# First k on ScalarE's DMA queue, second q on the software queue, and S ahead of Y, at the head of a fused retention and gated-MLP kernel

## The chip, the cores and the metric

One core of one Trainium2 chip. The metric is the device time of one execution in microseconds (us), median of several. A traced span is shorter than the time of the same execution (207.8 against 209.6 us for the kernel before).

## The reference

```python
# q, k, v: (4 batches, 8 heads, 768 steps, 64), fp32
gamma = 1.0 - 2.0 ** (-5.0 - np.arange(8))
for t in range(768):
    state = gamma * state + outer(k[t], v[t])      # per batch and head
    y[t] = q[t] @ state / 8
x = y as (3072, 512);  h = x @ w_in                # (512, 2048)
out = (h * cos(h)) @ w_out                         # (2048, 512)
```

The kernel works in chunks of 128 steps. A "pair" is one chunk of two batches (b = 0 and 1); there are 12 pairs. Per pair: convert q and k to bf16, transpose (T), form scores (A), multiply by the mask (M), form the output half by half (Y), update the state (S). Then comes the MLP: up-projection, h cos(h), down-projection.

## The kernel before

Lines with `clk.run` or `banks.give` are left out of these cuts without a mark. The loads at the start:

```python
load(nc.sync, 0, ("q0", "k0", "q1"))      # pair 0; SyncE's hardware queue, 256 KB each
nc.gpsimd.iota(...); nc.gpsimd.iota(...)
load(nc.gpsimd, 0, ("k1",))               # GpSimd's software queue
load(nc.gpsimd, 1, ("q0", "q1"))          # pair 1
load_k(1)
load(nc.gpsimd, 0, ("v0", "v1"))
# ... cut: constants ...
load(nc.gpsimd, 1, ("v0", "v1"))
load_w_in_0(); load_w_in(1)
# ... GpSimd converts most of the v of pairs 0 and 1 (vs) ...
```

The work on pair 0 (`warm(n)` issues n filler matmuls of 128x512 on zeros; `clk.run` only steers a model that picks PSUM banks, it issues nothing):

```python
warm(8)
conv_q(0, nc.vector, (0,))       # VectorE: q of b = 0 to bf16
conv_k(0, True)                  # ScalarE: k of b = 0, then of b = 1
stage_t(0, 0, 2)                 # PE: 4 transposes of q, 2 fillers, 4 of k; VectorE copies the bank out, "evicts" it (qkt)
conv_q(0, nc.vector, (1,))       # VectorE: q of b = 1, "the second q"
warm(3)
stage_m(0, stage_a(0, 0))        # A on PE, mask multiplies (am) on VectorE
# ... cut ...
```

The end of the head, and the first matmuls of the MLP:

```python
stage_m(1, stage_a(1, 0))
half_y(0, 0)
stage_m(1, stage_a(1, 1))
stage_s(0, nc.scalar.copy)       # S of pair 0, then its state copies (stb) on ScalarE
half_y(0, 1)
warm(3)
half_y(1, 0)                     # needs stb and am of pair 1
half_y(1, 1)
stage_s(1, nc.scalar.copy)
first_f()                        # first up-projection
```

## Time and profile before

| | before |
|---|---|
| time, first 3 runs | 209.31 us (209.24 to 209.52) |
| traced span | 207.8 us |
| first up-projection matmul | 16.94 us |
| from there to the end | 190.9 us |

From the page of the kernel before, part 1 (busy us, share of the span, count of instructions):

```profile
PE 200.2 (96%) x1646; PEld 112.9 (54%) x1646; DVE 113.3 (55%) x188; ACT 114.3 (55%) x193; POOL 102.2 (49%) x118
```

The waits of PE from 16.9 us to the end, kernel before; after these two header lines the list is empty:

```profile
core 0 of [0], span 207.8 us
engine line waited for: us in total, times, longest us
```

So PE is an unbroken stream from the first up-projection on. What can be won by this change lies in the first 17 us, and it is won only if that matmul starts earlier.

The timeline of the kernel before (start us, duration us, engine, line, operation, tiles, count, and in brackets the idle time before it with what ended it), VectorE:

```profile
3.91 0.69 DVE L195 TENSOR_TENSOR qk<-qf,gq 128x512 bf16<-128x512 f32 x1 [1.23 <-DMA qf<-in_q_dram]
7.42 0.69 DVE L214 TENSOR_SCALAR qkt<-bank 128x512 uint32<-128x512 uint32 x1 [2.81 <-PE bank L230]
8.02 0.68 DVE L195 TENSOR_TENSOR qk<-qf,gq 128x512 bf16<-128x512 f32 x1
...
13.41 2.47 DVE L266 TENSOR_TENSOR am<-bank,mask 128x512 bf16<-128x512 f32 x4
```

The first line is the first q, the second the first eviction of transposes, the third the second q. From 7.42 us no VectorE instruction has a bracket: it never idles until the last mask multiply ends at 13.41 + 2.47 = 15.88 us. I call this VectorE's chain. Its start was held by the first k, as ScalarE's timeline shows:

```profile
6.31 1.14 ACT L208 CAST qk<-kf 128x512 bf16<-128x512 f32 x2 [1.86 <-DMA kf<-in_k_dram]
...
14.44 1.19 ACT L313 CAST stb<-st_ps 64x512 bf16<-64x512 f32 x2
```

PE at the end of the head, kernel before (L301 is S, L413 fillers, L279 and L284 the Y halves, L360 the first up-projection):

```profile
13.95 0.44 PE L301 MATMUL st_ps<-vs,qk 128*64 128x64 bf16 x16
14.23 0.39 PE L284 MATMUL bank<-am,vs 128*64 128x128 bf16 x8
14.55 0.82 PE L413 MATMUL bank<-gt 128*128 128x512 bf16 x3
15.30 0.61 PE L279 MATMUL bank<-qkt,stb 128*64 128x128 bf16 x2
...
16.54 0.47 PE L301 MATMUL st_ps<-vs,qk 128*64 128x64 bf16 x16
16.94 0.30 PE L360 MATMUL bank<-xt,w_in 128*128 128x256 bf16 x1
```

The state copies end at 15.63 us, and the Y halves of pair 1 run behind them. Between the end of VectorE's chain and the up-projection lie 16.94 - 15.88 = 1.06 us.

The DMA queues between 4 and 5 us, kernel before (q0 is the software queue, with packets of up to 4 KB; q1 is SyncE's hardware queue, with 256-byte packets):

```profile
q0 software_dynamic: 62, 0.22, 72.1%
q1 hardware_dynamic: 254, 0.06, 27.9%
```

### The profile page before, as it was taken

How to read it: one execution, taken by the hardware profiler on the slowest of the kernel's cores; microseconds unless marked ns; L12 is line 12 of the kernel's file. 1: busy time of each engine (PE TensorE's matmuls, PEld its weight loads, DVE VectorE, ACT ScalarE, POOL GpSimd, SP SyncE). 2: the span in 40 equal slices, each digit the busy share in tenths (PEclk: the TensorE clock that was granted, in tenths of full speed). 3: DMA queues.
4: the chain of work that ended last, by engine and by line, in shares of the span. 5: the costliest groups of instructions: out<-in, count | busy, mean ns of one | idle time of the engine just before them, and what ended most of it. 6: DMA issues, size and time to landing. Idle time of an engine off the chain costs nothing.

```text
span 207.8 us, 4176 instructions
## 1 busy us (share of the span) xinstructions
PE 200.2 (96%) x1646; PEld 112.9 (54%) x1646; DVE 113.3 (55%) x188; ACT 114.3 (55%) x193; POOL 102.2 (49%) x118
## 2 busy tenths in 40 slices
PE   7689999999999999999999999999999999999993
PEld 2257554558897555546544465544465444444452
DVE  4591984464957563869874367853357244443000
ACT  6677873247997336577743754653554653553120
POOL 8999238399999999999995230000000000000000
PEclk9999999999999999999999999999999999999999
DMA  6999999999999999859899841161101101110212
GB/s 159 340 245 200 216 248 286 331 256 344 243 240 293 271 247 263 246 191 225 245 178 102 234 83 50 57 101 50 50 3 50 50 14 40 50 52 18 83 75 80
DMA packets 36644, 33.83 MB, mean 163 GB/s; under 512 B 26768, under 2 KB 29072, under 8 KB 36624
## 3 DMA queue, kind: packets, MB, share of 16 engines
q0 software_dynamic: 7808, 20.98, 39.6%
q1 hardware_dynamic: 28672, 12.49, 26.7%
q8 instruction: 13, 0.21, 0.5%
q10 hardware_dynamic: 144, 0.10, 0.1%
q14 instruction: 7, 0.06, 0.1%
HBM read 27.26 MB, written 6.29 MB: 161 GB/s over the span
## 4 chain that ended last, share of the span: by engine, by line
PE 92%; DVE 3%; DMA 2%; issue 1%; ACT 1%; SPq 0%; DVEq 0%
PE bank L379 39%; PE bank L338 32%; PE bank L349 7%; PE bank L257 3%; PE bank L279 3%; PE bank L284 3%; DMA kf<-in_k_dram 2%; PE bank L396 2%; PE st_ps L301 1%; DVE am L266 1%; PE bank L230 1%; PE bank L360 1%; PE bank L367 1%; DVE qkt L214 1%; DVE qk L195 1%
## 5 line engine op out<-in xcount | busy, mean ns | idle before, releaser
L331 DVE TENSOR_TENSOR gt<-bank,cosb 128x512 bf16<-128x512 f32 x96 | 64.8, 688 | 61.9 <-ACT cosb L327 61.6
L327 ACT ACTIVATE cosb<-bank,halfpi 128x512 bf16<-128x512 f32 x96 | 65.2, 688 | 49.9 <-PE bank L338 45.4
L379 PE MATMUL bank<-w_out_sb,gt 128*128 128x512 bf16 x368 | 89.6, 379 | 0.0
L338 PE MATMUL bank<-xt,w_in 128*128 128x512 bf16 x304 | 75.3, 380 | 0.0
L379 PEld LDWEIGHTS <-gt 128*128 128x128 bf16 x368 | 35.5, 98 | 41.2
L338 PEld LDWEIGHTS <-w_in 128*128 128x128 bf16 x304 | 33.7, 114 | 30.9
L266 DVE TENSOR_TENSOR am<-bank,mask 128x512 bf16<-128x512 f32 x48 | 30.4, 681 | 3.9 <-PE bank L257 3.9
L386 ACT COPY ob<-bank 128x512 f32<-128x512 f32 x23 | 13.4, 587 | 18.3 <-PE bank L379 18.3
L202 POOL TENSOR_TENSOR vs<-vf,gk 128x512 bf16<-128x512 f32 x21 | 21.4, 1042 | 3.2 <-PE st_ps L301 3.1
L132 POOL DMA_DIRECT2D vf<-in_v_dram x23 | 20.2, 883 | 5.2 <-DMA w_out_sb<-in_moe_w_out_dram 5.2
L195 POOL TENSOR_TENSOR qk<-qf,gq 128x512 bf16<-128x512 f32 x18 | 18.5, 1049 | 7.7 <-issue 4.8
L132 POOL DMA_DIRECT2D kf<-in_k_dram x21 | 18.9, 900 | 1.8 <-DMA w_out_sb<-in_moe_w_out_dram 1.6
L208 ACT CAST qk<-kf 128x512 bf16<-128x512 f32 x24 | 13.8, 615 | 9.5 <-DMA kf<-in_k_dram 9.5
L288 ACT CAST xt<-bank 128x512 bf16<-128x512 f32 x24 | 13.0, 588 | 8.0 <-PE bank L284 7.8
L132 POOL DMA_DIRECT2D qf<-in_q_dram x18 | 16.2, 901 | 0.6 <-DMA w_in<-in_moe_w_in_dram 0.6
L349 PE MATMUL bank<-xt,w_in 128*128 128x256 bf16 x128 | 14.7, 273 | 0.0
L349 PEld LDWEIGHTS <-w_in 128*128 128x128 bf16 x128 | 13.8, 114 | 0.4
L284 PE MATMUL bank<-am,vs 128*64 128x128 bf16 x192 | 11.7, 220 | 0.0
L279 PEld LDWEIGHTS <-stb 128*64 128x64 bf16 x160 | 8.8, 109 | 4.3 <-issue 3.1
L279 PE MATMUL bank<-qkt,stb 128*64 128x128 bf16 x160 | 10.7, 222 | 0.1
L284 PEld LDWEIGHTS <-vs 128*64 128x64 bf16 x192 | 10.0, 110 | 0.5 <-issue 0.4
L313 DVE CAST stb<-st_ps 64x512 bf16<-64x512 f32 x12 | 8.2, 684 | 2.7 <-PE st_ps L301 2.6
(46 smaller groups left out, 85.8 us busy)
## 6 DMA issues: line engine op xcount, KB each, us to landing
vf<-in_v_dram POOLq DMA_DIRECT2D x23, 256.0 KB, 6.5
out_dram<-ob SPq DMA_DIRECT2D x23, 256.0 KB, 2.2
kf<-in_k_dram POOLq DMA_DIRECT2D x21, 256.0 KB, 6.7
qf<-in_q_dram POOLq DMA_DIRECT2D x18, 256.0 KB, 5.6
w_out_sb<-in_moe_w_out_dram POOLq DMA_DIRECT2D x4, 512.0 KB, 12.7
qf<-in_q_dram SPq DMA_DIRECT2D x6, 256.0 KB, 8.3
w_in<-in_moe_w_in_dram POOLq DMA_DIRECT2D x3, 512.0 KB, 7.9
kf<-in_k_dram POOLq DMA_DIRECT2D x1, 512.0 KB, 6.0
```

The lines of the kernel that those rows point to most:

```text
L132: eng.dma_start(out=t[SLOT[p]][b], in_=src[2 * bp + b, :, ds(c * C, C)].rearrange("h t d -> t h d"))
L195: eng.tensor_tensor(out=qk[p % NB][:, b, 0], in0=qf[SLOT[p]][b], in1=bc(gq, p % NC), op=ALU.mult)
L202: eng.tensor_tensor(out=vs[p % NB][:, b], in0=vf[SLOT[p]][b], in1=bc(gk, p % NC), op=ALU.mult)
L208: nc.scalar.copy(out=qk[p % NB][:, b, 1], in_=kf[SLOT[p]][b])
L266: nc.vector.tensor_tensor(out=am[p % 2][b][j], in0=ap[j], in1=mask.unsqueeze(1).to_broadcast([128, HP, 128]), op=ALU.mult)
L279: nc.tensor.matmul(yp[ts(j, 64), a, :], lhsT=stb[p % 2][:, b, a, ts(j, 64)], rhs=qt(n, b, a), start=True, stop=False, skip_group_check=True)
L284: nc.tensor.matmul(yp[ts(j, 64), a, :], lhsT=vs[n][:, b, 2 * a + j, :], rhs=am[p % 2][b][j][:, a, :], start=(c == 0), stop=True, skip_grou ...
L327: nc.scalar.activation(out=cb, in_=bank, func=AF.Sin, bias=halfpi)
L331: nc.vector.tensor_tensor(out=out, in0=bank, in1=cb, op=ALU.mult)
L338: nc.tensor.matmul(bank, lhsT=w_in_t(i, f), rhs=xt[g % 2][:, i, :], start=(i == 0), stop=(i == KIN - 1))
L349: nc.tensor.matmul(bank[:, ts(e, 256)], lhsT=w_in_t(i, f + e), rhs=xt[g % 2][:, i, ts(hf, 256)], start=(i == 0 and e == 0), stop=(i == KIN ...
L379: nc.tensor.matmul(bank, lhsT=gt[g % 2][:, f, ts(j, 128)], rhs=w_out_sb[:, f, :], start=(f == 0), stop=(f == KOUT - 1))
```

## The change

Its intent: bring the first k sooner, by issuing it from ScalarE beside the first q; let the second q take the software queue and the first q of pair 1 the free place on SyncE's; and run S of pair 0 early, so that its state copies are done before the Y halves of pair 1 need them.

```diff
-    load(nc.sync, 0, ("q0", "k0", "q1"))
+    load(nc.scalar, 0, ("k0",))
+    load(nc.sync, 0, ("q0",))
+    load(nc.sync, 1, ("q0",))
@@
-    load(nc.gpsimd, 0, ("k1",))
-    load(nc.gpsimd, 1, ("q0", "q1"))
+    load(nc.gpsimd, 0, ("k1", "q1"))
+    load(nc.gpsimd, 1, ("q1",))
@@
     stage_m(1, stage_a(1, 0))
+    stage_s(0, nc.scalar.copy)
+    clk.run("pe", 0.0, 13.0)
+    stage_m(1, stage_a(1, 1))
     half_y(0, 0)
-    clk.run("pe", 0.0, 12.4)
-    stage_m(1, stage_a(1, 1))
-    stage_s(0, nc.scalar.copy)
     half_y(0, 1)
-    warm(3)
+    warm(1)
     half_y(1, 0)
+    warm(2)
     banks.give(spare, clk.pe)
     half_y(1, 1)
     stage_s(1, nc.scalar.copy)
```

## The prediction

> **What bounds the kernel now.** By the page's busy shares PE is busy 96% of 207.8 us. The waits of PE list none after 16.9 us: from there PE is one unbroken stream. So the change can only move the start of that stream, the first up-projection matmul at 16.94 us; a microsecond won there is a microsecond of total.
>
> **What bounds the first 17 us.** The timeline shows: k of batch 0 is second on SP's queue and lands at about 6.3 us. ScalarE copies it (0.62 us), PE transposes, and at 7.42 us VectorE starts. From 7.42 to 15.88 us VectorE never idles (fourteen conversions, evictions and mask multiplies of 0.68 us): the bound in the middle. PE has 1.06 us of work behind the last mask multiply: the second Y half of pair 1 and its S. The state copies on ScalarE (14.44 to 15.63 us) also hold the first Y half of pair 1 back to 15.67 us.
>
> **What the change does.**
> 1. k0 goes to a second hardware queue beside q0. The DMA view gives the hardware queue 1849 packets of 256 bytes by 4.0 us, so the two (2048 packets) are nearly through when the software queue's 4 KB packets begin (62 in the next microsecond, 254 for the hardware queue). The Trainium skill, page "DMA: Bandwidth & Descriptors", section "Queues, rings and completion order", says that the engines round-robin between queues packet by packet; the trace agrees: those 62 packets took 72% of the engines. I expect q0 later (4.3 to 5.2 us against 3.9), k0 earlier (4.6 to 5.8 against 6.3), and the first eviction of transposes at 6.2 to 7.0 us instead of 7.42.
> 2. The second q moves from third on the hardware queue (used at 8.02 us) to second on the software queue. The second software transfer was used by ScalarE at 8.00 us before. Its landing, about 7.9 us, then holds VectorE's second conversion, which stands in order ahead of the mask multiplies. So most of point 1 turns into idle time of VectorE. Net shift of its chain: 0.1 us, between -0.3 and +0.7.
> 3. S of pair 0 ahead of Y: state copies end at about 14.95 us instead of 15.63, so the first Y half of pair 1 runs before VectorE's last mask multiply ends. Behind that end remain the second half (0.45 us) and S (0.4 us): 0.85 instead of 1.06 us, a gain of 0.2 us.
>
> Sum: 0.3 us, and a little in case point 2 lands early.
>
> **Predicted time: 208.9 us**, 8 in 10 between 208.2 and 209.5. Chances: faster by over 2% 0.01 (4.2 us out of a 17 us head), within 2% 0.98, slower 0.01.
>
> **What would show it.** In the timeline: k's first copy before 6 us; first eviction of transposes before 7.1 us; VectorE then idle until the second q's DMA releases it at about 7.9 us, and unbroken to about 15.8 us; state copies done by 15 us; first up-projection matmul at about 16.6 us; no PE wait after it.
>
> **What would make it wrong.** If the second q lands on the software queue at 7 us, the chain gains up to 0.8 us. If it comes at 8.5 us or later, the change loses. If three queues in turn delay q0 beyond 6 us, point 1 gains nothing. If the new order of bank use makes PE wait, point 3's gain is lost.

## The result, and the profile after

The changed kernel took 209.03 us (median of 6, 208.88 to 209.78), the kernel before 209.38 us (median of 6). The ratio is 0.9989, 95% interval 0.9968 to 1.001. A ratio here is the mean time of one kernel's runs over that of the other's of the same rounds, so it is not quite the ratio of the medians quoted. Executions over 1.5% slower than the fastest of the same kernel are left out of the means. The interval holds 1; a later set of rounds (e0 below) gave 0.9981, 0.9968 to 0.9994, a gain of about 0.2%, whose interval does not hold 1.

| | before | after |
|---|---|---|
| first q converted from | 3.91 us | 4.49 us |
| first k copied from | 6.31 us | 4.92 us |
| first eviction (start of the chain) | 7.42 us | 7.16 us |
| second q converted from | 8.02 us | 7.77 us |
| end of VectorE's chain | 15.88 us | 15.64 us |
| first up-projection matmul | 16.94 us | 16.67 us |
| from there to the end | 190.9 us | 190.9 us |

Both profiled executions were slower than the medians of their kernels: 209.60 us against 209.38 before, 209.35 against 209.03 after. The table compares two single executions, and its 0.27 us at the last matmul agrees with the 0.35 us of the medians only roughly.

From the page of the kernel after, part 1:

```profile
PE 199.5 (96%) x1624; PEld 113.5 (55%) x1646; DVE 113.3 (55%) x188; ACT 114.1 (55%) x193; POOL 102.3 (49%) x118
```

(1624 matmuls against 1646 weight loads: some records are missing. The waits of PE after 16.6 us list only four gaps without a releaser, of 0.2 us at most, where they fell out.)

VectorE's timeline, kernel after:

```profile
4.49 0.69 DVE L197 TENSOR_TENSOR qk<-qf,gq 128x512 bf16<-128x512 f32 x1 [1.80 <-DMA qf<-in_q_dram]
7.16 0.69 DVE L216 TENSOR_SCALAR qkt<-bank 128x512 uint32<-128x512 uint32 x1 [1.98 <-PE bank L232]
7.77 0.68 DVE L197 TENSOR_TENSOR qk<-qf,gq 128x512 bf16<-128x512 f32 x1
...
13.16 2.48 DVE L268 TENSOR_TENSOR am<-bank,mask 128x512 bf16<-128x512 f32 x4
```

The first k came 1.39 us earlier, as its copy on ScalarE shows, and the state copies start 0.93 us earlier:

```profile
4.92 0.62 ACT L210 CAST qk<-kf 128x512 bf16<-128x512 f32 x1 [0.38 <-DMA kf<-in_k_dram]
...
13.51 1.18 ACT L315 CAST stb<-st_ps 64x512 bf16<-64x512 f32 x2 [1.78 <-PE st_ps L303]
```

Yet the first eviction moved by only 0.26 us. The k copy ended at 5.54 us, and PE transposed k only at 6.49 us. PE's timeline, kernel after (L415 are fillers, L232 transposes; the second transposes are those of k):

```profile
5.24 0.61 PE L232 MATMUL bank<-ident,qk 128*128 128x128 bf16 x4 [0.45 <-DVE qk L197]
5.64 1.06 PE L415 MATMUL bank<-gt 128*128 128x512 bf16 x2
6.49 0.63 PE L232 MATMUL bank<-ident,qk 128*128 128x128 bf16 x4
...
14.62 0.37 PE L281 MATMUL bank<-qkt,stb 128*64 128x128 bf16 x2 [0.25 <-DVE am L268]
...
15.31 0.60 PE L415 MATMUL bank<-gt 128*128 128x512 bf16 x2
15.85 0.25 PE L281 MATMUL bank<-qkt,stb 128*64 128x128 bf16 x2
...
16.32 0.42 PE L303 MATMUL st_ps<-vs,qk 128*64 128x64 bf16 x16
16.67 0.52 PE L362 MATMUL bank<-xt,w_in 128*128 128x256 bf16 x3
```

Two fillers stood between the transposes of q and those of k and took 1.06 us by their modelled ends (the transposes of k started 0.85 us after the first filler), because PE was still at its slow pace: 0.43 us from one filler to the next, against 0.22 us later. The slow pace is that of PE's granted clock. The views print a clock of 1.00 for every stage, but they count time without a clock record as full; the record itself, which I read from the packed trace, has its first entry (full clock) at 7.18 us here and at 4.23 us in the kernel before, and the pace rises at these moments. And at the end the first Y half of pair 1 did run before the chain's end, but two fillers then filled PE until 15.85 us, 0.2 us beyond that end. Behind the chain lie 16.67 - 15.64 = 1.03 us, against 1.06 before.

The DMA queues between 4 and 5 us, kernel after (q10 is ScalarE's hardware queue):

```profile
q1 hardware_dynamic: 831, 0.21, 93.2%
q10 hardware_dynamic: 305, 0.07, 33.5%
q0 software_dynamic: 2, 0.01, 2.0%
```

The software queue moved 62 packets in this microsecond before, 2 after. Its first packet came at 4.91 instead of 3.96 us. Still the second q, second in that queue, had landed at 7.28 us (I read landings from the semaphore events of the trace), where before, third on the hardware queue, it landed at 7.51 us.

### The profile page after: what moved, and what is told of

It reads as the page before. It is cut to its first block, busy times and chain, and to the rows that moved or that the text cites. A ratio compares the mean times of both kernels' runs of the same rounds, so it can differ in the third digit from the quotient of the medians.

```text
span 207.6 us, 4155 instructions
## 1 busy us (share of the span) xinstructions
PE 199.5 (96%) x1624; PEld 113.5 (55%) x1646; DVE 113.3 (55%) x188; ACT 114.1 (55%) x193; POOL 102.3 (49%) x118
## 4 chain that ended last, share of the span: by engine, by line
PE 91%; DVE 4%; DMA 2%; issue 1%; DVEq 0%
PE bank L381 38%; PE bank L340 32%; PE bank L351 7%; PE bank L281 3%; PE bank L259 3%; PE bank L286 2%; DMA qf<-in_q_dram 2%; DVE am L268 2%; PE bank L398 2%; PE bank L232 1%; PE st_ps L303 1%; DVE qk L197 1%; DVE qkt L216 1%; PE bank L362 1%; PE bank L369 1%
## 5 line engine op out<-in xcount | busy, mean ns | idle before, releaser
L381 PE MATMUL bank<-w_out_sb,gt 128*128 128x512 bf16 x359 | 88.5, 379 | 0.7 <-issue 0.3
L340 PE MATMUL bank<-xt,w_in 128*128 128x512 bf16 x294 | 74.3, 380 | 0.7 <-issue 0.3
L351 PE MATMUL bank<-xt,w_in 128*128 128x256 bf16 x128 | 14.7, 273 | 0.0
```

The source lines that it names most:

```text
L340: nc.tensor.matmul(bank, lhsT=w_in_t(i, f), rhs=xt[g % 2][:, i, :], start=(i == 0), stop=(i == KIN - 1))
L351: nc.tensor.matmul(bank[:, ts(e, 256)], lhsT=w_in_t(i, f + e), rhs=xt[g % 2][:, i, ts(hf, 256)], start=(i == 0 and e == 0), stop=(i == KIN ...
L381: nc.tensor.matmul(bank, lhsT=gt[g % 2][:, f, ts(j, 128)], rhs=w_out_sb[:, f, :], start=(f == 0), stop=(f == KOUT - 1))
```

## The experiments

Twelve kernels in three sets of four, five rounds each, each set on one chip. All results were correct. Medians come from 5 or 6 runs. "First F" is the start of the first up-projection matmul; "behind" is First F less the end of VectorE's chain. Ratios are to the kernel before in the same set.

| run | second q converted | chain's end | First F | behind | time us | ratio (95%) |
|---|---|---|---|---|---|---|
| e0 the change again | 7.83 | 15.70 | 16.73 | 1.03 | 208.96 | 0.9981 (0.9968-0.9994) |
| e1 loads only | 7.17 | 15.04 | 16.09 | 1.05 | 208.80 | 0.9981 (0.9968-0.9995) |
| e2 order only | 7.85 | 15.72 | 16.75 | 1.03 | 209.36 | 1.0001 (0.9989-1.0013) |
| e3 no fillers in T | 7.30 | 15.17 | 16.21 | 1.04 | 208.86 | 0.9978 (0.9966-0.9990) |
| e5 e3, second q on SyncE | 6.80 | 14.68 | 16.22 | 1.54 | 208.86 | 0.9958 (0.9920-0.9997) |
| e6 e3, one hardware queue | 7.46 | 15.33 | 16.37 | 1.04 | 209.20 | 0.9978 (0.9935-1.0021) |
| e7 e3, no end fillers | 7.43 | 15.31 | 16.09 | 0.78 | 208.65 | 0.9948 (0.9909-0.9987) |
| e8 e3, S of pair 1 ahead | 7.16 | 15.04 | 15.57 | 0.53 | 208.42 | 0.9939 (0.9900-0.9977) |
| e9 e8 and e5 together | 6.76 | 14.88 | 15.62 | 0.74 | 208.20 | 0.9950 (0.9927-0.9974) |
| e10 e8, S of pair 0 late | 7.11 | 14.98 | 16.04 | 1.06 | 208.86 | 0.9980 (0.9957-1.0004) |
| e11 change, one more filler | 7.44 | 15.31 | 16.34 | 1.03 | 208.91 | 0.9982 (0.9957-1.0008) |
| e12 e9, weights later | 6.73 | 15.01 | 16.40 | 1.39 | 208.31 | 0.9960 (0.9934-0.9987) |

The columns from the trace are of one execution each, the times of five or six. In the later two sets the kernel before scattered widely (up to 211.7 us, and 215.5 us in one run, which the ratios leave out), so the medians say more there than the ratios, and a difference between sets of less than about 0.2 us should not be trusted.

### e0: the change again

Edit: none.

> The changed kernel unaltered, for a second profile and a tighter interval. Theory P (PE's fillers): the first eviction of transposes starts at 7.16 us in the first profile because PE, still at its slow pace, has two filler matmuls (1.06 us) between the transposes of q and those of k; where PE reaches its fast pace earlier in this execution the eviction starts up to 0.5 us earlier. Theory Q (second q): the second q's landing sets the start of VectorE's second conversion. Both: about 0.3 us below the kernel before, first up-projection matmul at 16.3 to 16.7 us. It also tells whether the software queue's first packets come at 4.9 us again (3.9 us in the kernel before).

Measured: 208.96 us. The profile repeats the first one: fillers at 5.82 and 6.24 us, 0.42 us apart, first eviction at 7.23 us, First F at 16.73 us. But this profiled execution was the slowest of its five: 209.41 us, the others 208.85 to 209.00. In the first set too the profiled one took 209.35 us and four of the others 208.9 to 209.1 (the fifth 209.78). So both profiles of the changed kernel show an execution with a late pace (clock record from 7.18 and 6.93 us), and most executions were about 0.4 us faster. That these had their fast pace early is an inference: they have no trace.

### e1: the loads only

Edit: the change's new loads in the kernel before.

> The new loads with the old order of PE's work. If the two parts add up as predicted, VectorE's second conversion starts at about 7.8 us, its chain ends at about 15.6 us, and the first up-projection matmul at about 16.7 us: 0.25 us below the kernel before, the same as the whole change, since the order alone would only save PE work behind the chain's end. If the order carries the gain, 16.9 us and no gain.

Measured: 208.80 us, First F at 16.09 us. In this execution PE was fast at 5.34 us, so the fillers cost little, and VectorE did what the prediction said, waiting for the second q. VectorE's timeline of e1:

```profile
6.20 0.69 DVE L216 TENSOR_SCALAR qkt<-bank 128x512 uint32<-128x512 uint32 x1 [1.17 <-PE bank L232]
7.17 0.69 DVE L197 TENSOR_TENSOR qk<-qf,gq 128x512 bf16<-128x512 f32 x1 [0.28 <-DMA qf<-in_q_dram]
```

Only it landed at 7.14 us, not 7.9. The loads carry the whole gain of the change: 208.80 us without the new order, 208.96 with it, in the same set. The expected 16.7 us was missed because the chain came 0.6 us earlier than I thought. Its runs also fall into two groups: 208.74 to 208.82 (four) and 209.26, 209.34 (two).

### e2: the order only

Edit: the change's new order of PE's work with the old loads.

> The old loads with the new order of PE's work. Predicted 0.2 us of gain: state copies done by about 15.0 us, the first Y half of pair 1 before VectorE's last mask multiply ends (15.9 us), first up-projection matmul at about 16.75 us. Rival: the two fillers between the Y halves (0.60 us, and 0.54 us from their start to the next matmul in the changed kernel) give the gain back, and it starts at 16.9 us, no gain.

Measured: 209.36 us against 209.26 for the kernel before, ratio 1.0001. The rival was right: behind the chain lie 1.03 us, no fewer than before. First F came at 16.75 us, as the theory said, but for another reason: the chain itself came 0.16 us earlier in this execution than in the first profile of the kernel before. VectorE's timeline of e2 shows more:

```profile
6.27 0.69 DVE L214 TENSOR_SCALAR qkt<-bank 128x512 uint32<-128x512 uint32 x1 [1.72 <-PE bank L230]
7.85 0.69 DVE L195 TENSOR_TENSOR qk<-qf,gq 128x512 bf16<-128x512 f32 x1 [0.89 <-DMA qf<-in_q_dram]
```

With the same old loads as the kernel before, the first k was there at 5.16 us instead of 6.31, and the chain still did not start earlier than 7.85 us: it waited for the second q. In the old loads the second q was a bound close behind the first k, so a faster k alone could move the second conversion from 8.02 us only to 7.85 us (here) or about 7.5 us (the second q's landing in the first profile). The new loads brought both: the second q landed at 7.1 to 7.5 us on the software queue, against 7.5 and 7.8 us as third on the hardware queue.

### e3: no fillers between the first transposes

```diff
-    stage_t(0, 0, 2)
+    stage_t(0, 0)
```

> The changed kernel without the two filler matmuls between the first transposes of q and of k. Theory P: the first eviction starts at about 6.1 us instead of 7.16, VectorE's second conversion then waits for the second q until about 7.3 us, and the first up-projection matmul comes at about 16.2 us, 0.4 to 0.5 us earlier than in the changed kernel. Theory Q: the second conversion stays at 7.8 us and nothing moves. A loss would mean that PE stays at its slow pace for longer without the fillers.

Measured: 208.86 us, and all five runs within 208.85 to 208.98; First F at 16.21 us. VectorE's timeline of e3:

```profile
6.29 0.69 DVE L216 TENSOR_SCALAR qkt<-bank 128x512 uint32<-128x512 uint32 x1 [1.11 <-PE bank L232]
7.30 0.69 DVE L197 TENSOR_TENSOR qk<-qf,gq 128x512 bf16<-128x512 f32 x1 [0.32 <-DMA qf<-in_q_dram]
```

Theory P holds for the profiled executions of the change: the fillers delayed the chain. Theory Q holds for what comes next: without them VectorE waits for the second q (whether that also holds First F, e5 tests). In the median e3 wins only 0.1 us over e0 (208.96). No run of e3 is near 209.4 us, but with five runs, against one such in five of e0 and two of 209.3 us or more in six of the first set, it is not shown that the slow group is gone.

### e5: the second q back on SyncE's queue

```diff
-    load(nc.sync, 1, ("q0",))
+    load(nc.sync, 0, ("q1",))
-    load(nc.gpsimd, 0, ("k1", "q1"))
-    load(nc.gpsimd, 1, ("q1",))
+    load(nc.gpsimd, 0, ("k1",))
+    load(nc.gpsimd, 1, ("q0", "q1"))
```

> Against e3 (no fillers between the first transposes) only the two second-rank q tiles change places: the second q of pair 0 goes second on SP's hardware queue, where the other tile landed at 5.8 us, and the first q of pair 1 goes to the software queue, where the other landed at 7.3 us. Theory Q (with the fillers gone the second q's landing binds VectorE): its second conversion starts right behind the first eviction, at about 6.9 us instead of 7.30, and the first up-projection matmul comes at about 15.8 us instead of 16.20; time about 208.5 us. Rival: GpSimd's conversions of the values (done at 14.65 us in e3) or the transposes of pair 1 (their q now lands later) hold the chain, and it comes at 16.1 to 16.2 us.

Measured: 208.86 us, First F at 16.22 us: nothing won, although VectorE's chain started at once (second q at 6.80 us, right behind the eviction) and ended 0.5 us earlier than in e3. The rival was right. Waits of PE from 12 to 17 us in e5:

```profile
PE st_ps L303 <- POOL vs L204: 0.3, 1, 0.3
```

S of pair 0 waited for GpSimd's conversion of the first v until 12.71 us; behind it stand the state copies (13.06 to 14.24 us), the first Y half, the two fillers (14.87 us) and the second Y half with S. This row, not VectorE, is the bound here, and it gives First F within 0.01 us of e3's. In e3 the state copies, too, ran from 13.05 us and the fillers from 14.85 us, so there the row stood as late, though VectorE's chain ended 0.49 us later.

### e6: one hardware queue

```diff
-    load(nc.scalar, 0, ("k0",))
-    load(nc.sync, 0, ("q0",))
+    load(nc.sync, 0, ("q0", "k0"))
     load(nc.sync, 1, ("q0",))
```

> Against e3 only the first k goes back to SP's queue, second behind q, with the first q of pair 1 third; the second q stays second on the software queue. Theory A (the second hardware queue brings k early and lets the hardware transfers finish before the software ones): k lands between 5.1 and 6.3 us as in the two profiles with the old loads, the software queue's first packets come at 3.9 us again instead of 4.95, the second q lands at about 7.9 us instead of 7.28, and the first up-projection matmul comes at 16.7 to 16.9 us instead of 16.20. Theory B (what helps the second q is its place in the software queue alone, not the second hardware queue): it lands at 7.3 us and the matmul comes at 16.2 to 16.3 us.

Measured: 209.20 us, First F at 16.37 us. The DMA queues between 4 and 5 us in e6:

```profile
q0 software_dynamic: 64, 0.25, 85.3%
q1 hardware_dynamic: 218, 0.05, 23.7%
```

Neither theory is right as a whole. As A says, the software queue is back at 64 packets (its first at 3.92 us). As B says, the second q landed at 7.43 us, hardly later than the 7.28 us of e3, and inside the 7.1 to 7.5 us that the second place in the software queue gave in all the other runs that had it. And the first k, second in SyncE's queue, was there at 4.68 us, no later than by its own queue. The three profiles with k second on SyncE's queue have it at 4.68, 5.16 and 6.31 us; the eleven with k on ScalarE's queue have it at 4.7 to 5.1 us. In these traces, then, the second hardware queue made the first k's arrival steady more than it made it early. This one trace does not show that B holds: the second transfer of the software queue, whichever tile it was, landed at 7.43, 7.81 and 7.91 us in the three traces with one hardware queue (e6, e2, before) and at 7.1 to 7.5 us in the eleven with two. And the queue is worth something in time: all six runs of e6 (209.14 to 209.57 us) are slower than all six of e5 (208.84 to 208.99), in the same set, and than all five of e3 (208.85 to 208.98, another set), from which it differs by this queue alone. Of the 0.27 us between the profiled executions of e6 and e5 0.15 us lie before First F, 0.04 behind it and 0.08 outside the traced span.

### e7: no fillers between the Y halves

```diff
     half_y(1, 0)
-    warm(2)
```

> Against e3 only the two fillers between the two Y halves of pair 1 go. In the changed kernel the second half starts 0.2 us after VectorE's last mask multiply ends, and 1.05 us lie between that end and the first up-projection matmul, as many as with the old order. Theory: the fillers' time (from 14.85 us in e3) gives the gain of the new order back; without them 0.85 us remain and the matmul comes at about 16.0 us instead of 16.20. Rival: it is the release by the last mask multiply and PE's own work that take 1.05 us; nothing moves.

Measured: 208.65 us. Behind the chain lie 0.78 us instead of 1.04. PE in e7:

```profile
15.72 0.44 PE L303 MATMUL st_ps<-vs,qk 128*64 128x64 bf16 x16
16.09 1.18 PE L362 MATMUL bank<-xt,w_in 128*128 128x256 bf16 x9
```

The fillers had taken back the gain of the new order: the 0.2 us that the prediction had for it appear once they are gone. First F came only 0.12 us earlier than in e3, since the second q came 0.13 us later in this execution; the time is 0.2 us lower.

### e8: S of pair 1 ahead of the last Y half

```diff
     half_y(1, 0)
-    warm(2)
+    stage_s(1, None)
     banks.give(spare, clk.pe)
     half_y(1, 1)
-    stage_s(1, nc.scalar.copy)
+    state_out(1, nc.scalar.copy)
```

> Against e3 the two fillers between the Y halves of pair 1 are replaced by S of pair 1, which needs no mask multiply; its state copies stay behind. Then only the second Y half (0.42 us) stands behind VectorE's last mask multiply: 0.5 to 0.65 us between its end and the first up-projection matmul instead of 1.05, which comes at 15.6 to 15.8 us instead of 16.20; time 208.3 to 208.5 us. Rival: the up-projection then waits for the copy of the second Y half by ScalarE, or PE meets another wait, and less than 0.2 us is won.

Measured: 208.42 us (all six runs 208.41 to 208.58), First F at 15.57 us, 0.53 us behind the chain. PE in e8:

```profile
14.70 0.43 PE L303 MATMUL st_ps<-vs,qk 128*64 128x64 bf16 x15
...
15.57 1.61 PE L362 MATMUL bank<-xt,w_in 128*128 128x256 bf16 x13
```

S needs no mask multiply, so it does useful work where the fillers stood, and only the last Y half remains behind VectorE. As expected; the rival fell.

### e9: e8 with the second q on SyncE's queue

Edit: those of e8 and e5 together.

> e8 with the second q second on SP's hardware queue, as in e5. If the second q's landing still bound e8 (its VectorE chain ends at 15.03 us), the chain ends at about 14.7 us and the first up-projection matmul comes at about 15.2 us instead of 15.56. If, as e5 suggests, GpSimd's conversion of the first values (which S of pair 0 waited for at 12.71 us in e5) is the next bound, with the state copies and the first Y half behind it, it comes at 15.4 to 15.6 us and the time stays within 0.15 us of e8's 208.42.

Measured: 208.20 us (208.19 to 208.32), First F at 15.62 us, at the upper edge of the second range expected; the time is 0.22 us under e8's, a little more than I allowed, in another set and on another chip. That difference is not won in the head, as First F comes 0.05 us later than in e8: of the 0.16 us between the profiled executions 0.11 lie behind First F (190.99 us in e8, 190.88 in e9) and the rest outside the traced span. PE's S of pair 0 again waited for GpSimd until 12.76 us, and in this execution the k of pair 1 came late, too (its copy at 10.09 us, 9.46 in e8). It has the lowest median of all: ratio 0.9950 to the kernel before. Whether it truly beats e8 is open, the two did not share rounds; both beat the kernel before and, by medians of 208.4 or less against 208.96 and 209.03, the change.

### e10: e8 with S of pair 0 in its old place

```diff
-    stage_s(0, nc.scalar.copy)
-    clk.run("pe", 0.0, 13.0)
-    stage_m(1, stage_a(1, 1))
     half_y(0, 0)
+    clk.run("pe", 0.0, 12.4)
+    stage_m(1, stage_a(1, 1))
+    stage_s(0, nc.scalar.copy)
     half_y(0, 1)
```

> e8 with S of pair 0 back in its old place, behind Y and A. It tells whether the new order is worth anything once the work behind the last mask multiply is small. Theory: the state copies then end about 0.6 us later (15.0 instead of 14.25 us), the first Y half of pair 1 and S of pair 1 come behind VectorE's end, and the first up-projection matmul comes 0.3 to 0.5 us later than in e8, at about 15.9 to 16.05 us, time 208.7 to 208.9 us. Rival: the order is worth nothing here either; 15.6 us and 208.4 us.

Measured: 208.86 us, First F at 16.04 us, as the theory said. PE in e10 had to wait for the state copies:

```profile
14.78 0.24 PE L281 MATMUL bank<-qkt,stb 128*64 128x128 bf16 x1 [0.36 <-ACT stb L315]
```

Behind the chain lie 1.06 us again, against 0.53 in e8. So the new order is worth about 0.45 us once S of pair 1 has been moved too (e10 and e8 are of different sets), and nothing in the change as it stands.

### e11: one more filler at the start

```diff
-    warm(8)
+    warm(9)
```

> The changed kernel with nine filler matmuls instead of eight at the start. In both profiles of the changed kernel PE sat idle for about half a microsecond before the transposes of the first q and was still at its slow pace (0.43 us from one filler to the next) until about 6.9 us; with the new loads alone, where q came 0.15 to 0.3 us earlier, it was at its fast pace (0.22 us) at 5.3 us. Theory I (the idle gap keeps PE slow): the ninth filler closes most of the gap, PE is fast by about 5.3 us, the first eviction starts at about 6.2 us, VectorE's second conversion at the second q's landing (7.2 to 7.5 us), up-projection at about 16.2 us, and all executions lie near 208.9 us. Rival: the pace changes by a clock of its own, not by the gap; then executions near 209.4 us remain beside those near 208.9 us, or the profile shows slow fillers again.

Measured: 208.91 us. PE in e11:

```profile
3.73 1.49 PE L415 MATMUL bank<-gt 128*128 128x512 bf16 x3
5.10 0.61 PE L232 MATMUL bank<-ident,qk 128*128 128x128 bf16 x4
5.50 1.06 PE L415 MATMUL bank<-gt 128*128 128x512 bf16 x2
6.35 0.44 PE L232 MATMUL bank<-ident,qk 128*128 128x128 bf16 x4
```

Theory I falls. PE did not idle before the transposes of q (no bracket), and the two fillers behind them still took 1.06 us; the pace rose only at about 6.4 us. In e5, on the other hand, PE idled for 0.6 us before these transposes (5.39 us), and they ran at the fast pace. Over all profiles the clock record's first entry begins between 4.04 us (e10) and 7.20 us (e12), with fillers from 1.2 us in all of them, and the fillers' pace rises with it. Each first entry lasts 201.39 or 204.80 us, which is 59 or 60 times 3.413 us: the clock changes on steps of about 3.4 us, and where they fall differs from run to run. That fits the rival, a clock of its own. It is what the Trainium skill states, "TensorE: Matmul & The Clock Gate", section "Part 1: The HAM clock gate (the "warmup" mystery)": the rate doubles after about 3.4 us of activity, judged in a window that runs freely, so that the moment varies from run to run. The runs agree with the doubling (0.43 to 0.22 us per filler), with the step and with the variation; from the first filler to the rise it took 2.8 to 6.0 us here. All six times lie near 208.9 us even so; this execution lost only about 0.25 us to its fillers, since the second q landed at 7.17 us.

### e12: second block of weights issued later

```diff
     load_w_in_0()
-    load_w_in(1)
@@
     conv_v(0, nc.gpsimd, (1,))
+    load_w_in(1)
     conv_v(1, nc.gpsimd)
```

(on top of e9)

> e9 with the issue of the second block of input weights (0.78 us on GpSimd) moved behind GpSimd's conversions of the first values. If those conversions are the bound in e9, S of pair 0 runs about 0.3 us earlier (first values converted at about 12.3 instead of 12.6 us) and the first up-projection matmul comes 0.2 to 0.3 us earlier than in e9. Rival: the values land too late (10.5 and 11.3 us) or the conversions of pair 1, which now end later, hold S of pair 1: nothing is won, or up to 0.4 us is lost. The weights themselves should land when they did, since the software queue works them off in order.

Measured: 208.31 us, no gain over e9 in the same set. The profiled execution (209.18 us) was far slower than the other five (208.18 to 208.42), so its trace speaks for a bad case only: PE fast at about 7.2 us, GpSimd waiting for v, not for its own issues, and PE's S of pair 1 waiting for GpSimd:

```profile
POOL vs L426 <- DMA vf<-in_v_dram: 0.9, 1, 0.9
```

```profile
15.70 0.32 PE L303 MATMUL st_ps<-vs,qk 128*64 128x64 bf16 x8 [0.28 <-POOL vs L204]
```

Both parts of the rival fit this execution: v had landed at 10.96 us, and the conversions of pair 1, with the issue now ahead of them, ended at 15.65 us and held S of pair 1 and with it First F. In the other traces v landed between 10.1 and 10.9 us and GpSimd's issues ended at 11.0 us, so the first conversions could start earlier in good executions; the times show no gain. A likely reason, not shown by a trace of such an execution: the issue and the conversions together take GpSimd as long as before, and in e9 S of pair 1 (from 14.77 us) already ran close behind their end (14.7 us).

## Why the prediction was right or wrong

**The total was right** (208.9 us predicted, 209.03 measured, within 208.2 to 209.5), in part by luck, as the terms show. Its ground was right too: no PE wait after the first up-projection, and every microsecond there is one of the total. In all traces the rest took 190.9 to 191.0 us, whatever the head.

**Point 1, k beside q: half right.** The arrivals were right (q 4.49 us, k 4.92 us). The first eviction was predicted at 6.2 to 7.0 us and came at 7.16 us. The step that failed is one the text does not contain: that PE would transpose k when k was there. Two fillers stood between in PE's program and ran first although k was there (its copy ended at 5.54 us), and at the slow pace they took 1.06 us. Without them (e3), or with an early fast pace (e1), the eviction came at 6.2 to 6.3 us. In the trace of the kernel before, on which the prediction rests, they had cost nothing: PE was fast by then (0.59 us for two) and, above all, waiting for k anyway.

**Point 2, the second q: right mechanism, mis-sized term.** "Its landing, about 7.9 us" measured 7.1 to 7.5 us. I took the second software transfer's landing from the kernel before, where it shared the engines with three hardware transfers until 7.1 us; in the changed kernel the hardware transfers were through by 5.5 us. That this is the cause is not shown: in e6 the hardware transfers again ran until 7.0 us, and the second q landed at 7.43 us. VectorE's wait for it is seen in e1, e3, e6, e7, e8 and e10, not in the profile of the change, where the fillers hid it. The chain's shift, predicted 0.1 us, was 0.2 and 0.25 us in the two profiles of the change, and 0.7 to 0.9 us in e1, e3 and e8 (measured against the 8.02 us of the kernel before, itself one execution).

**Point 3, S ahead: wrong.** "0.85 instead of 1.06 us, a gain of 0.2 us" measured 1.03 us. The state copies ended early, as predicted (14.69 us; 14.95 predicted), and the first Y half moved ahead, as predicted. But the fillers between the halves held the second half 0.2 us beyond the chain's end. e2 shows no gain from the order, e7 shows the 0.26 us that the fillers took back, e8 and e10 what the order can give.

So the sum came out right by two errors of opposite sign: more from the loads than predicted, nothing from the order. That they cancelled was luck. Of the intent of the change only the loads gave a gain, and not by the first k alone: with k early the second q was the bound (e2). How the gain divides between k's own queue and the second q's new place is not shown, since no run makes one of these moves alone with the fillers in place. Each seems to matter: e6, which differs from e3 by k's own queue alone, loses 0.34 us to it in the median (in another set, and as much to e5 in its own), and e2, with k early by chance, still waits for the second q.

Left open: why the software queue's first packet comes 1 us later whenever two hardware queues are in use, how the gain divides between the two moved loads, and what share of untraced executions has the late pace.

## What to carry to other kernels

Fillers that keep the array busy are free only where PE would wait anyway: when a change makes their wait shorter, they become the wait, and useful work that is independent of the awaited result (here S of pair 1) should stand in their place. Before speeding up the transfer that ends an engine's idle time, look for the next operand in the same in-order queue: if it lands at nearly the same time, little is won. When a head of some microseconds decides, take several profiles: the same code gave an eviction at 6.2 or 7.2 us according to when PE's pace rose.

## What the Trainium skill lacked or had wrong

- "DMA: Bandwidth & Descriptors", section "Queues, rings and completion order", says that each engine takes turns between queues packet by packet, and its section "Issuing engines are not separate DMA queues" that issuing from several engines only saves issue time. Lacking: with one hardware queue in use the software queue's first packets came at 3.9 to 4.0 us (3 of 3 traces), with two at 4.7 to 5.0 us (11 of 11), for the same bytes and the same issue times of the software transfers; between 4 and 5 us it moved 57 to 64 packets in the one case and 0 to 12 in the other. Nor do the turns show as one packet each: in the kernel before 254 hardware packets stood beside 62 software ones between 4 and 5 us (what a trace lists as a packet may not be the page's packet). No run settles the cause.
- The same page does not say how much an arrival scatters where 256-byte and 4 KB packets share the engines: the first k, second in its hardware queue, was there at 4.68, 5.16 or 6.31 us in three executions; on a queue of its own at 4.7 to 5.1 us.
- "TensorE: Matmul & The Clock Gate" gives the moment of the fast pace as about 4 us into activity, give or take 0.5 us. Here it lay between 2.8 (e10) and 6.0 us (e12) after the first filler at 1.2 us, and e11, which closed an idle gap of about 0.45 us, still had it at 5.3 us. A note in the same section allows more, 6, 11 or 14 slow matmuls in runs of one kernel; it is the half microsecond that is too narrow.
